# Token blocks of 480 columns that run across batch ends, in a kernel of polysketch attention followed by a SwiGLU block

## The chip, the cores and the metric

The kernel runs on one core of one Trainium2 chip. The metric is device time in microseconds (us), the median of several runs; lower is better. The profile is one execution of the same kernel, recorded by the hardware. Its engines are called PE (TensorE, matrix products), PEld (TensorE's weight loads), DVE (VectorE), ACT (ScalarE), POOL (GpSimd) and SP (SyncE, which here only issues DMAs).

## The reference

Attention with polynomial sketches, without a softmax, and then a gated feed-forward block over all tokens:

```python
batch, n_heads, seq, head_dim = (4, 4, 1088, 32)      # r = 8
def phi(x):
    a = np.einsum('rd,bhsd->bhsr', S1, x)
    b = np.einsum('rd,bhsd->bhsr', S2, x)
    return np.einsum('bhsi,bhsj->bhsij', a, b).reshape(*x.shape[:-1], r * r)
q_p, k_p = (phi(q), phi(k))
kv = np.einsum('bhsf,bhsd->bhfd', k_p, v)
z = np.sum(k_p, axis=2)
num = np.einsum('bhsf,bhfd->bhsd', q_p, kv)
den = np.einsum('bhsf,bhf->bhs', q_p, z)[..., None] + 1e-06
...
x = attn_out.transpose(0, 2, 1, 3).reshape(4352, 128)
g = x @ w_gate                        # 128 x 1536
silu = g * (1.0 / (1.0 + np.exp(-g)))
val = x @ w_val
out = (silu * val) @ w_out            # 1536 x 128
```

## The kernel before, in words

All tokens lie in `xT`, 128 model dimensions by 4352 token columns, 1088 for each of the four batches. Attention fills it batch by batch, and the feed-forward part reads it in blocks of columns. A *unit* is one block with one of the twelve chunks of 128 hidden features: gate product, value product, silu, product of the two (a tile of `hbuf`). The *down* product (`down`, L966, its matmul at L972) adds up the twelve hidden tiles of a block in one PSUM bank, `acc`, some five units later. `store` (L997) then transposes the sum on DVE (L1001) and issues one output DMA for each of the four groups of 32 features (L1007).

Each batch is cut into blocks of 384, 384 and 320 columns (`plan`, L65). Batch 0 goes through attention and the feed-forward part first, with plain FP32 products (`unit`, L933, matmuls at L941). The loop at L1240 runs the other three batches: nine blocks, 108 units, counted by `y`; `line` (L964) is the order of the blocks. The last of the line has 384 columns, of which the last 128 are multiplied the other way round at the very end (`straight`, L985, matmul at L987).

In that loop most products are *cut* (`cut_unit`, L889): tokens and weights are split into parts of fewer bits so that three faster F32R matmuls replace one FP32 matmul. One of them (L898) makes a small correction that ACT copies out of PSUM (L902); two more (L906, L907) accumulate the main part, which DVE adds to the correction (L908). Then ACT applies silu (L914) and POOL multiplies gate and value (L919). With `both=True` gate and value are cut. Otherwise only the value is, and the gate is one FP32 matmul (L900). The prediction calls the first kind *both* and the second *single*. Before, a unit is both from `y=26` (`GATES`) on and at y = 11, 14, 17, 20 and 23.

`cut_tokens` (L861) makes the parts of a block's tokens in three steps, x1 on ACT (L869), x0 on POOL or DVE (L870), and xd on DVE (L874); `cut_weights` (L828) does the same for weights, and its last gate part is the tile `gphq` (L859). In the loop `cut_tokens` is called in two halves, nine and four units before a block's first unit; the second half is xd.

PSUM has eight banks. `bank` and `pair` take the ones that were used longest ago and are not held; a both unit takes two pairs of the three that are left.

Attention of the later batches is written as a generator (`attentions`, L603) whose steps `parts_of` takes between units, by a rule on `y` (L1255). Its larger groups of matmuls wait at a `yield "pe"` until `group()` starts them, at the units listed in `GROUPS`. For batch 2: values and key sketches, then query sketches; for batch 3: numerators of batch 2 (L770) and values (L376), then query sketches (L330); last the numerators of batch 3. `numerators` copies its result into `xT` (L787). The steps between are DVE work above all: `query_step` (L732) makes the denominators (L737 to L743), multiplies query features (`phq`, L365) and transposes them (L752) into `phT`, which the numerators need.

Each engine works through its instructions in the order in which the code issues them.

Of the kernel before, what the change touches and what calls it, by code (L numbers as in the profile page):

```python
# [19 lines left out]
def kernel(  # L20
# [44 lines left out]
    plan = [(HX + 2 - s) // 3 for s in range(3)]  # L65
    XS = plan[0]
    steps = [(sum(plan[:s]), n) for s, n in enumerate(plan)]
    blocks = [(S * b + 64 * x0, 64 * n) for b in range(B) for x0, n in steps]
    BW = 64 * XS

    LAST = len(blocks) - 2
    SPLIT = BW - P

    thirds = [(c, c + 3) for c in range(0, NCH, 3)]
    pieces = dict.fromkeys(("wg", "wv"), [(0, 1), (1, 3)] + thirds[1:])
# [223 lines left out]

    NH = 27  # L300
    hbuf = const.tile([P, NH, BW], FP32, name="hbuf")
    slots = list(range(NH))
    slot_of = {}

    xT = const.tile([P, NT], FP32, name="xT")
# [297 lines left out]
    def attentions():  # L603

        yield from turn_keys(1)
        yield from turn_queries(1)
        hold("a")
        kp = wide("a")  # L610
        for i, c in enumerate(kpieces):
            key_products(kp[:, i, :], *c)
        ka = apool.tile([P, NC * H, R], FP32, tag="kas", name="kas")

        def sketch(ps, i):
            c0, c1 = kpieces[i]
            return ps[:, i, 0 : 64 * (c1 - c0)].rearrange("p (x t r) -> p x t r", t=2, r=R)

        for i, (c0, c1) in enumerate(kpieces):
            nc.scalar.copy(ka[:, H * c0 : H * c1, :], sketch(kp, i)[:, :, 0, :])  # L620
        phk = apool.tile([P, NC, H, R, R], FP32, tag="phk", name="phk")
        for n, (i, c0, c1) in enumerate(((0, 0, 3), (0, 3, 5), (1, 5, 7), (1, 7, 9))):
            first = H * (c0 - kpieces[i][0])
            kb = sketch(kp, i)[:, first : first + H * (c1 - c0), 1, :]
            key_features(phk, (ka[:, H * c0 : H * c1, :], kb), c0, c1)
            if n == 3:
                release("a")
            if n % 3 != 1:
                yield
        zs, sums = feature_sums(phk)  # L630
        for f in sums:
            f()
        yield from turn_keys(2)
        kvz = wide("a")
        values(kvz[:, 0, :], phk, zs)
        kab, kcopies = sketched(wide("b"), key_products, 2, "kab2")
        fold(kvz[:, 0, :])
        spread = spread_out(1, kvz[:, 0, :])
        hold("a", "b")
        yield  # L640
        qab, copies = sketched(wide("a"), query_sketches, 3, "qab")
        run_copies(copies, 2)
        yield
        run_copies(kcopies, 2)
        release("a", "b")
        for n, _ in enumerate(query_step(1, qab)):
            if n % 2 == 0:
                yield
        yield
        yield  # L650
        numerators(1, spread)
        yield "first"

        phk = apool.tile([P, NC, H, R, R], FP32, tag="phk", name="phk")
        yield from features(phk, kab)
        zs, sums = feature_sums(phk)
        for f in sums:
            f()
        yield from turn_keys(3)
        yield from turn_queries(2)  # L660
        for b in (2, 3):
            yield "pe"
            if b == 3:
                numerators(2, spread)
            hold("a")
            kv = bank()
            kv_bank = [max(used, key=used.get)]
            release("a")
            values(kv, phk, zs)
            if b == 2:  # L670
                kab, copies = sketched(wide("a"), key_products, 2, "kab2")
                run_copies(copies, 2)
            fold(kv)
            spread = spread_out(b, kv)
            touch(*kv_bank)
            yield
            yield "pe"
            qab, copies = sketched(wide("b"), query_sketches, 3, "qab")
            run_copies(copies, 2)
            yield  # L680
            if b == 2:
                yield from turn_queries(3)
                phk = hbuf[:, NH - 6 :, :].rearrange("p s (n h i j) -> p (s n) h i j", h=1, i=R, j=R)
                phk = phk.rearrange("p (c h) o i j -> p c (h o) i j", h=H)
                yield from features(phk, kab)
                zs, sums = feature_sums(phk)
            yield from beside(query_step(b, qab), sums)
        yield "pe"
        numerators(3, spread)
        yield  # L690
# [39 lines left out]
    turned = {}  # L730

    def query_step(b, qab):  # L732
        phq = apool.tile([P, NC, H, R, R], FP32, tag="phqs", name="phq")
        phT = turned[b] = apool.tile([P, H, 2, NC, 32], FP32, tag="phk", name="phT")
        dot = apool.tile([P, NC * H, R], FP32, tag="dot", name="dot")
        den = apool.tile([P, NC * H], FP32, tag="den", name="den")
        nc.vector.tensor_tensor(  # L737
            out=dot[:], in0=qab[:, 1, :, :], in1=qab[:, 2, :, :], op=ALU.mult
        )
        nc.vector.tensor_reduce(out=den[:], in_=dot[:], axis=AX.X, op=ALU.add)  # L740
        nc.vector.tensor_scalar_add(den[:], den[:], 1e-6)
        nc.vector.reciprocal(den[:], den[:])
        nc.vector.tensor_tensor(  # L743
            out=qab[:, 0, :, :], in0=qab[:, 0, :, :],
            in1=den[:].unsqueeze(2).to_broadcast([P, NC * H, R]), op=ALU.mult,
        )
        yield
        for c0, c1 in fpieces:
            x = slice(H * c0, H * c1)
            key_features(phq, (qab[:, 0, x, :], qab[:, 1, x, :]), c0, c1)  # L750
            yield
            nc.vector.transpose(  # L752
                out=phT[:, :, :, c0:c1, :].rearrange("p h g c t -> p c (h g) t"),
                in_=phq[:, c0:c1, :, :, :].rearrange(
                    "p c h (g i) j -> p c (h g) (i j)", g=2
                ),
            )
            yield
# [102 lines left out]
    def cut_tokens(i, engine=nc.gpsimd):  # L861
# [1 line left out]
        t0, n = blocks[i]  # L863
        x = xT[:, t0 : t0 + n]
        x1, x0, xd = x_parts[i] = [
            apool.tile([P, BW], F32R, tag=tag, name=name, bufs=2)
            for tag, name in (("qb", "x1"), ("dT", "x0"), ("rd", "xd"))
        ]
        nc.scalar.activation(x1[:, 0:n], x, AF.Copy, scale=CUT)  # L869
# [11 lines left out]
    def doubles(k):  # L881

        if room[1] + k > 2:
            room[:] = fpool.tile([P, 2, BW], FP32, tag="sgl", name="sum", bufs=4), 0
        at = room[1]
        room[1] += k
        return room[0][:, at : at + k, :]

    def cut_unit(i, j, both=False):  # L889
# [20 lines left out]
        )  # L910

        def last():
            sg = fpool.tile([P, BW], FP32, tag="sg", name="sg", bufs=5)[:, 0:n]
            nc.scalar.activation(sg, sums[:, 0] if both else g, AF.Silu)  # L914
            slot_of[i, j] = slots.pop(0)
            hj = hbuf[:, slot_of[i, j], :]
            hidden[i, j] = hj
            todo.append((i, j))
            nc.gpsimd.tensor_tensor(out=hj[:, 0:n], in0=sg, in1=sums[:, len(ws) - 1], op=ALU.mult)  # L919
# [13 lines left out]
    def unit(i, j, late=False, between=(None, None)):  # L933
# [4 lines left out]
        for o, w in ((g, wg), (u, wv)):  # L938
# [2 lines left out]
            nc.tensor.matmul(  # L941
                o[:, 0:n], w[:, j, :], xT[:, t0 : t0 + n], start=True, stop=True
            )
        sg = doubles(1)[:, 0, :] if late else fpool.tile([P, BW], FP32, tag="sg", name="sg", bufs=5)
        nc.scalar.activation(sg[:, 0:n], g[:, 0:n], AF.Silu)  # L945
        slot_of[i, j] = slots.pop(0)
        hj = hbuf[:, slot_of[i, j], :]
        hidden[i, j] = hj
        todo.append((i, j))
        if late:  # L950
# [10 lines left out]
        o, sg = lates.pop(0)  # L961
        nc.gpsimd.tensor_tensor(out=o, in0=o, in1=sg, op=ALU.mult)

    line = [3 * b + k for b in range(1, B) for k in ((0, 2, 1) if b == B - 1 else range(3))]  # L964

    def down():  # L966

# [17 lines left out]
    def straight(ps, j):  # L985

        nc.tensor.matmul(  # L987
            ps,
            hidden.pop((LAST, j))[:, SPLIT:BW],
            wo[:, j, :],  # L990
            start=(j == 0),
            stop=(j == NCH - 1),
        )
# [3 lines left out]
    def store(i, n):  # L997
        t0 = blocks[i][0]

        o = fpool.tile([P, BW // 32, 32], FP32, tag="o", name="o", bufs=2)  # L1000
        nc.vector.transpose(  # L1001
            out=o[:, 0 : n // 32, :], in_=acc.pop(i)[:, 0:n].rearrange("p (x t) -> p x t", t=32)
        )
        b, x0 = divmod(t0 // 32, NX)
        for a in range(4):
            queue = nc.scalar if i == LAST and a % 2 else nc.sync
            queue.dma_start(  # L1007
                out=rows[b, a, :, x0 : x0 + n // 32, :],
                in_=o[32 * a : 32 * a + 32, 0 : n // 32, :],
            )  # L1010

    keep_warm(98, 32)
    keep_warm(12, 64)
# [205 lines left out]
        parts_of(1)  # L1221
    run(x_steps or cut_tokens(HEAD, nc.vector))

    slots[:] = range(NH - 10)

    END = len(line) * NCH
    GROUPS, GATES = (5, 7, 26, 28, 52), 26

    token_steps = {}
    for m, i in enumerate(line[1:], 1):
        gen = cut_tokens(i)
        for at in (NCH * m - 9, NCH * m - 4):
            token_steps.setdefault(at, []).append(gen)
    oldest[0] = True
    hold("acc")
# [2 lines left out]
    for y in range(END):  # L1240
# [5 lines left out]
        if y == END - 1:  # L1246
            finish()
            unit(i, j)
        else:
            cut_unit(i, j, both=y >= GATES or (y > 10 and y % 3 == 2))  # L1250
        for _ in range(2):

            if len(todo) > min(5 + (todo[0] == (line[1], 0)), END - y + 1):
                down()
        parts_of(y < 8 or (y % 3 != 2 if y < GATES else y % 3 == 0))  # L1255
        if y == 0:
            gate_rows = cut_weights(wg, lows, nc.vector)
        for n, row in enumerate(gate_rows):
# [47 lines left out]
```

## Time and profile before

| what | value |
|---|---|
| median of 3 runs | 289.59 us (289.50 to 289.62) |
| span of the profiled execution | 287.6 us |
| granted TensorE clock | 1.000 |
| loop over later batches: first L898 to last L987 | 92.8 to 283.9 us |
| busy in it: DVE from 92.8 to 142.0 | 42.8 of 49.2 us |
| busy from 192.0 to 284.1 | DVE 55.9 of 92.1 us |
| HBM read, written | 11.41 MB, 2.23 MB |

The costliest groups of instructions of the loop, from the page's fifth part (columns: line, engine, operation, out<-in with partitions x elements, count, then busy us and mean ns, then the idle time of the engine before them and what ended it):

```profile
L919 POOL TENSOR_TENSOR hbuf<-sg,sum 128x384 f32<-128x384 f32 (+1 forms) x107 | 107.6, 1011 | 59.0 <-ACT sg L914 54.7
L908 DVE SCALAR_TENSOR_TENSOR sum<-PS,sum 128x768 f32<-128x768 f32 (+3 forms) x107 | 88.5, 830 | 46.7 <-ACT sum L902 41.0
L972 PE MATMUL PS<-hbuf,wo 128*128 128x384 f32 (+2 forms) x288 | 103.7, 459 | 0.0
L902 ACT ACTIVATE sum<-PS 128x768 f32<-128x768 f32 (+3 forms) x107 | 76.5, 714 | 43.7 <-PE PS L898 40.0
```

TensorE's matmuls overlap in the record (the next one starts before the one before has ended), so their durations are longer than their share of the time; the spacing of their starts is what they cost. An FP32 matmul shows as two halves.

### The profile page before, as it was taken

The numbers are of one execution on the slowest core, as the hardware profiler recorded it, in microseconds if no ns is written. First come the engines' busy times: TensorE is split into PE (matmuls) and PEld (weight loads), VectorE is DVE, ScalarE is ACT, GpSimd is POOL, SyncE is SP. The second block draws the span as 40 slices with busy tenths as digits, with TensorE's granted clock in tenths as the row PEclk, the third lists the DMA queues.
The fourth block names the chain that finished last, engine by engine and source line by source line (L and its number), as shares of the span: only waits on it lengthen the run. The fifth ranks groups of instructions, "written<-read, shape, count | busy, mean of one in ns | idle before, by whom it ended". The sixth has DMA issues, their size and how long they took to land.

```text
span 287.6 us, 6035 instructions
## 1 busy us (share of the span) xinstructions
PE 278.8 (97%) x2308; PEld 212.1 (74%) x2308; DVE 205.8 (72%) x337; ACT 173.3 (60%) x347; POOL 162.3 (56%) x183
## 2 busy tenths in 40 slices
PE   7899999999999999999998999999999999999995
PEld 7545566666666776777776888868888988889984
DVE  3997988884576979998548888746656567575651
ACT  3567565723402866665556787757777776777760
POOL 3315322279401894889924686555666676766660
PEclk9999999999999999999999999999999999999999
DMA  6574293212311213010001001001001010010101
GB/s 190 162 217 112 57 287 108 89 68 82 95 25 26 64 52 84 0 28 0 2 16 29 2 0 23 2 0 31 0 0 27 2 24 1 2 27 1 18 7 27
DMA packets 26141, 14.32 MB, mean 50 GB/s; under 512 B 19840, under 2 KB 24192, under 8 KB 26112
## 3 DMA queue, kind: packets, MB, share of 16 engines
q1 hardware_dynamic: 25456, 13.84, 18.7%
q8 instruction: 18, 0.29, 0.4%
q10 hardware_dynamic: 656, 0.10, 0.2%
q14 instruction: 11, 0.09, 0.1%
HBM read 11.41 MB, written 2.23 MB: 47 GB/s over the span
## 4 chain that ended last, share of the span: by engine, by line
PE 88%; DVE 6%; DMA 1%; ACT 1%; issue 1%; SPq 0%; DVEq 0%; ACTq 0%
PE PS L972 26%; PE PS L941 16%; PE PS L898 11%; PE PS L906 10%; PE PS L907 10%; PE PS L900 4%; PE PS L770 2%; PE PS L342 2%; PE PS L330 2%; PE PS L376 2%; DVE sum L908 1%; DMA kld<-in_k_dram 1%; PE PS L987 1%; DVE gphq L859 1%; PE PS L485 1%
## 5 line engine op out<-in xcount | busy, mean ns | idle before, releaser
L919 POOL TENSOR_TENSOR hbuf<-sg,sum 128x384 f32<-128x384 f32 (+1 forms) x107 | 107.6, 1011 | 59.0 <-ACT sg L914 54.7
L908 DVE SCALAR_TENSOR_TENSOR sum<-PS,sum 128x768 f32<-128x768 f32 (+3 forms) x107 | 88.5, 830 | 46.7 <-ACT sum L902 41.0
L972 PE MATMUL PS<-hbuf,wo 128*128 128x384 f32 (+2 forms) x288 | 103.7, 459 | 0.0
L902 ACT ACTIVATE sum<-PS 128x768 f32<-128x768 f32 (+3 forms) x107 | 76.5, 714 | 43.7 <-PE PS L898 40.0
L972 PEld LDWEIGHTS PS<-hbuf,wo 128*128 128x128 f32 x288 | 51.8, 189 | 9.8 <-issue 0.4
L898 PE MATMUL PS<-xd,gphq 128*128 128x384 f32 (+1 forms) x86 | 49.6, 576 | 1.7 <-DVE sum L908 1.3
L914 ACT ACTIVATE sg<-sum 128x384 f32<-128x384 f32 (+1 forms) x86 | 42.4, 493 | 5.5 <-DVE sum L908 5.3
L906 PE MATMUL PS<-x,w 128*128 128x384 f32 (+1 forms) x107 | 41.0, 384 | 0.0
L898 PE MATMUL PS<-xd,wd 128*128 128x384 f32 (+1 forms) x107 | 38.1, 356 | 0.2 <-DVE xd L874 0.2
L907 PE MATMUL PS<-x,wb 128*128 128x384 f32 (+1 forms) x107 | 35.1, 328 | 0.0
L941 PE MATMUL PS<-xT,wg 128*128 128x384 f32 (+1 forms) x74 | 29.5, 480 | 0.0
L941 PE MATMUL PS<-xT,wv 128*128 128x384 f32 (+1 forms) x74 | 28.8, 471 | 0.2 <-DVE wv L276 0.2
L906 PE MATMUL PS<-x,graw 128*128 128x384 f32 (+1 forms) x86 | 28.1, 326 | 0.2 <-ACT xT L787 0.2
L898 PEld LDWEIGHTS PS<-xd,wd 128*128 128x128 f32 x107 | 20.3, 190 | 10.5 <-issue 0.7
L907 PE MATMUL PS<-x,graw 128*128 128x384 f32 (+1 forms) x86 | 28.0, 326 | 0.0
L945 ACT ACTIVATE sg<-PS 128x384 f32<-128x384 f32 (+1 forms) x31 | 14.4, 467 | 21.3 <-PE PS L941 19.6
L898 PEld LDWEIGHTS PS<-xd,gphq 128*128 128x128 f32 x86 | 16.3, 189 | 12.3 <-DVE sum L908 2.3
L956 DVE TENSOR_TENSOR hbuf<-sg,PS 128x384 f32<-128x384 f32 (+1 forms) x31 | 16.2, 525 | 10.4 <-PE PS L941 10.1
L907 PEld LDWEIGHTS PS<-x,wb 128*128 128x128 f32 x107 | 20.1, 188 | 2.7
L906 PEld LDWEIGHTS PS<-x,w 128*128 128x128 f32 x107 | 20.1, 188 | 2.7
L941 PEld LDWEIGHTS PS<-xT,wv 128*128 128x128 f32 x74 | 13.8, 190 | 9.2 <-DVE hbuf L956 0.9
L941 PEld LDWEIGHTS PS<-xT,wg 128*128 128x128 f32 x74 | 13.3, 189 | 9.3 <-issue 1.2
(131 smaller groups left out, 351.6 us busy)
## 6 DMA issues: line engine op xcount, KB each, us to landing
kld<-in_k_dram SPq DMA_DIRECT2D x4, 544.0 KB, 4.1
vld<-in_v_dram SPq DMA_DIRECT2D x12, 144.0 KB, 4.7
qld<-in_q_dram SPq DMA_DIRECT2D x3, 544.0 KB, 3.3
raw<-in_moe_w_out_dram SPq DMA_DIRECT2D x4, 384.0 KB, 4.6
out_dram<-o SPq DMA_DIRECT2D x28, 48.0 KB, 1.9
raw<-in_moe_w_gate_dram SPq DMA_DIRECT2D x3, 384.0 KB, 3.2
raw<-in_moe_w_val_dram SPq DMA_DIRECT2D x3, 384.0 KB, 3.5
out_dram<-o SPq DMA_DIRECT2D x16, 40.0 KB, 1.7
```

The source lines that it names most:

```text
L898: nc.tensor.matmul(ds[:, k], wd, xd, start=True, stop=True)
L900: nc.tensor.matmul(g, wg[:, j, :], xT[:, t0 : t0 + n], start=True, stop=True)
L902: nc.scalar.activation(sums, ds, AF.Copy, scale=-1.0 / BETA)
L906: nc.tensor.matmul(ps[:, k], w1, x1, start=True, stop=False)
L907: nc.tensor.matmul(ps[:, k], wb, x0, start=False, stop=True)
L908: nc.vector.scalar_tensor_tensor(out=sums, in0=ps, scalar=1.0 + 1.0 / BETA, in1=sums, op0=ALU.mult, op1=ALU.add)
L914: nc.scalar.activation(sg, sums[:, 0] if both else g, AF.Silu)
L919: nc.gpsimd.tensor_tensor(out=hj[:, 0:n], in0=sg, in1=sums[:, len(ws) - 1], op=ALU.mult)
L941: nc.tensor.matmul(o[:, 0:n], w[:, j, :], xT[:, t0 : t0 + n], start=True, stop=True)
L945: nc.scalar.activation(sg[:, 0:n], g[:, 0:n], AF.Silu)
L956: nc.vector.tensor_tensor(out=hj[:, 0:n], in0=sg[:, 0:n], in1=u[:, 0:n], op=ALU.mult)
L972: nc.tensor.matmul(acc[i][:, 0:n], wo[:, j, :], hidden[i, j][:, 0:n], start=(j == 0), stop=(j == NCH - 1),)
```

## The change

The later batches' 3264 columns are cut into blocks of 480 from column 1088 on, across the ends of batches: six of 480 and one of 384. Tiles of the loop grow from 384 to 480 columns (`WB`); hidden tiles are slices of 480 columns of the same `hbuf`, 13 in place of 17. A store whose block runs across a batch's end issues its DMAs for each batch. Attention's groups move from units 5, 7, 26, 28, 52 to 4, 6, 20, 22, 40, and the first both unit to 20, with none before. Steps of attention are taken at every unit before 20 and at every second one after. The tokens of the third and the fifth block are cut later than the others, at 20 and 22, and at 40 and 44, since they hold columns of a batch whose numerators come at 20 or 40. `query_step` has one more `yield`, after the sum of the denominators, and a `phq` tile of a third of the size, which the three pieces share; for batch 1 the rule `n % 2` is turned over, so that its steps come where they came before.

```diff
-    blocks = [(S * b + 64 * x0, 64 * n) for b in range(B) for x0, n in steps]
+    blocks = [(64 * x0, 64 * n) for x0, n in steps]
     BW = 64 * XS
-    LAST = len(blocks) - 2
-    SPLIT = BW - P
+    WB = 480
+    blocks += [(t, min(WB, NT - t)) for t in range(S, NT, WB)]
+    LAST = len(blocks) - 1
+    SPLIT = blocks[LAST][1] - P
...
-            if n % 2 == 0:
+            if n % 2 == 1:
                 yield
...
     def query_step(b, qab):
-        phq = apool.tile([P, NC, H, R, R], FP32, tag="phqs", name="phq")
...
         nc.vector.tensor_reduce(out=den[:], in_=dot[:], axis=AX.X, op=ALU.add)
+        yield
         nc.vector.tensor_scalar_add(den[:], den[:], 1e-6)
...
-            x = slice(H * c0, H * c1)
-            key_features(phq, (qab[:, 0, x, :], qab[:, 1, x, :]), c0, c1)
+            x, n = slice(H * c0, H * c1), c1 - c0
+            phq = apool.tile([P, NC // 3, H, R, R], FP32, tag="phqs", name="phq")
+            key_features(phq, (qab[:, 0, x, :], qab[:, 1, x, :]), 0, n)
...
-            apool.tile([P, BW], F32R, tag=tag, name=name, bufs=2)
+            apool.tile([P, WB], F32R, tag=tag, name=name, bufs=2)
...
-    line = [3 * b + k for b in range(1, B) for k in ((0, 2, 1) if b == B - 1 else range(3))]
+    line = list(range(HEAD, len(blocks)))
...
-        b, x0 = divmod(t0 // 32, NX)
-        for a in range(4):
+        t1 = t0 + n
+        while t0 < t1:
+            b, x0 = divmod(t0 // 32, NX)
+            m = min(t1 - t0, S * (b + 1) - t0) // 32
+            k = (t0 - blocks[i][0]) // 32
+            for a in range(4):
...
-    slots[:] = range(NH - 10)
+    flat = hbuf[:].rearrange("p s w -> p (s w)")
+    slots[:] = [flat[:, WB * k : WB * k + WB] for k in range((NH - 10) * BW // WB)]
...
-    GROUPS, GATES = (5, 7, 26, 28, 52), 26
+    GROUPS, GATES = (4, 6, 20, 22, 40), 20
...
-        for at in (NCH * m - 9, NCH * m - 4):
+        for at in {2: (20, 22), 4: (40, 44)}.get(m, (NCH * m - 9, NCH * m - 4)):
             token_steps.setdefault(at, []).append(gen)
...
-            cut_unit(i, j, both=y >= GATES or (y > 10 and y % 3 == 2))
+            cut_unit(i, j, both=y >= GATES)
...
-        parts_of(y < 8 or (y % 3 != 2 if y < GATES else y % 3 == 0))
+        parts_of(y < GATES or y % 2 == 0)
```

More of the change, by code (lines that the diff above doesn't have):

```diff
@@ L301 @@
     hbuf = const.tile([P, NH, BW], FP32, name="hbuf")
-    slots = list(range(NH))
+    slots = [hbuf[:, k, :] for k in range(NH)]
     slot_of = {}
@@ L753, in query_step @@
                 out=phT[:, :, :, c0:c1, :].rearrange("p h g c t -> p c (h g) t"),
-                in_=phq[:, c0:c1, :, :, :].rearrange(
+                in_=phq[:, 0:n, :, :, :].rearrange(
                     "p c h (g i) j -> p c (h g) (i j)", g=2
@@ L883, in doubles @@
         if room[1] + k > 2:
-            room[:] = fpool.tile([P, 2, BW], FP32, tag="sgl", name="sum", bufs=4), 0
+            room[:] = fpool.tile([P, 2, WB], FP32, tag="sgl", name="sum", bufs=4), 0
         at = room[1]
@@ L912, in last @@
         def last():
-            sg = fpool.tile([P, BW], FP32, tag="sg", name="sg", bufs=5)[:, 0:n]
+            sg = fpool.tile([P, WB], FP32, tag="sg", name="sg", bufs=5)[:, 0:n]
             nc.scalar.activation(sg, sums[:, 0] if both else g, AF.Silu)
             slot_of[i, j] = slots.pop(0)
-            hj = hbuf[:, slot_of[i, j], :]
+            hj = slot_of[i, j]
             hidden[i, j] = hj
@@ L943, in unit @@
             )
-        sg = doubles(1)[:, 0, :] if late else fpool.tile([P, BW], FP32, tag="sg", name="sg", bufs=5)
+        sg = doubles(1)[:, 0, :] if late else fpool.tile([P, WB], FP32, tag="sg", name="sg", bufs=5)
         nc.scalar.activation(sg[:, 0:n], g[:, 0:n], AF.Silu)
         slot_of[i, j] = slots.pop(0)
-        hj = hbuf[:, slot_of[i, j], :]
+        hj = slot_of[i, j]
         hidden[i, j] = hj
@@ L988, in straight @@
             ps,
-            hidden.pop((LAST, j))[:, SPLIT:BW],
+            hidden.pop((LAST, j))[:, SPLIT : SPLIT + P],
             wo[:, j, :],
@@ L998, in store @@
         t0 = blocks[i][0]
-        o = fpool.tile([P, BW // 32, 32], FP32, tag="o", name="o", bufs=2)
+        o = fpool.tile([P, WB // 32, 32], FP32, tag="o", name="o", bufs=2)
         nc.vector.transpose(
@@ L1003, in store @@
         )
-        b, x0 = divmod(t0 // 32, NX)
-        for a in range(4):
[L1006 to L1010, printed above, removed]
+        t1 = t0 + n
[4 more added lines that the diff above has]
+            for a in range(4):
+                queue = nc.scalar if i == LAST and a % 2 else nc.sync
+                queue.dma_start(
+                    out=rows[b, a, :, x0 : x0 + m, :],
+                    in_=o[32 * a : 32 * a + 32, k : k + m, :],
+                )
+            t0 += 32 * m
     keep_warm(98, 32)
```

## The prediction

> **What bounds the kernel now.** I read the page first: the busy shares, the slices, the chain's totals.
>
> ```profile
> PE 278.8 (97%) x2308; PEld 212.1 (74%) x2308; DVE 205.8 (72%) x337; ACT 173.3 (60%) x347; POOL 162.3 (56%) x183
> PE   7899999999999999999998999999999999999995
> DVE  3997988884576979998548888746656567575651
> PE 88%; DVE 6%; DMA 1%; ACT 1%; issue 1%; SPq 0%; DVEq 0%; ACTq 0%
> ```
>
> TensorE carries the end. Only its own work, or a wait that stops it, moves the time. So I split the stretch in which the diff works: from unit y=0 (first matmul of L898, 92.75 us) to the last matmul of L987 (283.9). I add up each unit's matmuls from the spacing of their starts. The chain in order of time gives the spacing; two steady units of 384 columns and two of 320:
>
> ```profile
> 174.61 0.65 PE PS L972 x2
> 176.30 0.65 PE PS L972 x2
> ...
> 160.33 0.54 PE PS L972 x2
> 161.76 0.54 PE PS L972 x2
> ```
>
> A unit with both products cut ("both") takes 1.69 us at 384 columns, 1.42 at 320. It is six F32R matmuls (two each of L898, L906, L907) and one FP32 matmul of L972, which the trace shows as two halves of 0.32 us. In the timeline neighbouring F32R starts are 0.1745 us apart at 384 and 0.1465 at 320; 6 x 0.1745 + 0.645 = 1.692 and 6 x 0.1465 + 0.538 = 1.417, so the parts agree with the whole. A unit with the gate uncut ("single") has three F32R and one more FP32 matmul (L900): 1.168 + 0.645 = 1.81 at 384.
>
> Before there are 19 singles of 384, 2 of 320, 52 boths of 384, 34 of 320 and the last unit in FP32 (1.935): 34.5 + 3.0 + 88.0 + 48.2 + 1.9 = 175.6 us. (The last block's shorter downs and the extra matmuls of L987 cancel; both kernels have them.) The stretch is 191.1. Of the other 15.5, attention's matmuls take 10.2 (2.35 and 1.81 at the first two groups, 4.5 at the next two, 1.5 at the last). About 5 is waiting. The waits of TensorE from 92 to 285 us name the visible part:
>
> ```profile
> PE PS L898 <- DVE sum L908: 1.3, 1, 1.3
> PE PS L330 <- DVE sum L908: 0.5, 1, 0.5
> PE PS L898 <- DVE gphq L859: 0.4, 1, 0.4
> PE PS L906 <- ACT xT L787: 0.2, 1, 0.2
> PE PS L898 <- DVE xd L874: 0.2, 1, 0.2
> ```
>
> Counted by unit length against the sums above, the losses are larger than these rows: 0.7 at y=11 (gphq), 1.0 at y=25 to 28 (second row included), 1.6 at y=32 (first row), 1.3 around the last group at y=52. The biggest is a block of five instructions on VectorE; its timeline and TensorE's next start:
>
> ```profile
> 154.10 0.86 DVE L737 TENSOR_TENSOR dot<-qab 128x288 f32<-128x288 f32 x1
> 154.99 0.45 DVE L740 TENSOR_REDUCE den<-dot 128x36 f32<-128x288 f32 x1
> 155.47 0.61 DVE L741 TENSOR_SCALAR den<-den 128x36 f32<-128x36 f32 x1
> 156.12 0.38 DVE L742 RECIPROCAL den<-den 128x36 f32<-128x36 f32 x1
> 156.53 0.46 DVE L743 TENSOR_TENSOR qab<-qab,den 128x288 f32<-128x288 f32 x1
> 157.78 0.41 PE L898 MATMUL PS<-xd,gphq 128*128 128x320 f32 x1 [1.31 <-DVE sum L908]
> ```
>
> For 2.9 us L908 cannot empty PSUM, and the units behind it find no bank.
>
> **What the Trainium skill says.** "TensorE: Matmul & The Clock Gate", section "Wait — 56ns, not 53.3ns?": warm starts are N / 2.4 GHz plus about 2.5 ns apart. The FP32 halves agree (768 / 2.4 = 320, measured 322). The F32R ones do not: 160 + 14.5 and 133.3 + 13, so the trace's numbers are used. "Perfetto Trace Analysis", section "Matmuls", says larger matmuls are more efficient; 14 ns a matmul is all that can be won here. "SBUF — State Buffer", section "SBUF: two separate sides": a VectorE instruction with two SBUF inputs and a GpSimd one exclude each other. The trace agrees: xd (two SBUF inputs) takes from 476 to 1358 ns:
>
> ```profile
> L874 DVE SCALAR_TENSOR_TENSOR xd<-x,x x9: 476/953/1358, 92.1 to 256.4; 128x384 fp32r<-128x384 f32 x6, 128x320 fp32r<-128x320 f32 x3
> ```
>
> **The change, part by part.**
> 1. *Seven blocks for nine.* 108 units become 84: y=0 to 19 single at 480, 20 to 71 both at 480, then 11 boths and the last at 384. No row shows 480 columns. An F32R matmul is at least 200 + 13 = 213 ns and at most, on the straight line through 146.5 and 174.5, 216.5; I take 215 (the rest grew little over 64 columns). An FP32 one: 4 x 480 / 2.4 + 5 = 805. Single 3 x 0.215 + 2 x 0.805 = 2.255, both 6 x 0.215 + 0.805 = 2.095. Sum: 45.1 + 108.9 + 18.6 + 1.9 = 174.6, so **-1.0** (-1.7 at 213, -0.45 at 216.5). It is small because uncut gates cover 9600 columns instead of 7936, each one array pass more: 1664 / 2.4 = 0.7 of a gross 1.7.
> 2. *No both before y=20.* The first need of gphq moves from y=11 to y=20, 45 us after y=0 instead of 21; L859 issues at the same y (6 to 9). The wait goes: **-0.7** (0.4 to 0.7).
> 3. *Denominators in two parts.* For batch 3, dot and reduce (1.31) now fall at y=22 and the rest (1.45) at y=24, each before another L908. A 480 unit gives VectorE 2.1 us against about 1.17 of L908 (0.822 at 640 and 0.954 at 768 elements, so 1.03 ns an element, with 960), so 1.3 fits before a bank is missed. But the tokens of the block from y=24 on now get their xd at y=22, in VectorE's queue straight behind dot and reduce. Counted from the start of unit 22: the copies of qab (1.14) hold ACT, L902 ends at 1.6, L908 at 2.8, dot and reduce at 3.7 to 4.1, xd at 4.4 to 5.4. Unit 24's first matmul wants it at 4.2. Estimated new wait 0.2 to 1.2, taken 0.8; the queue behind it (L908 of y=23) is wanted only at 6.3. Net 0.8 - 1.6 = **-0.8** (-1.5 to +0.4).
> 4. *Start.* x1, x0 and xd of the first block grow by 96 columns each, in one chain (0.52, 0.56, 0.55 at 384): 3 x 0.09, and TensorE already waits 0.18 there: **+0.3** (0.2 to 0.5).
> 5. *Groups at 4, 6, 20, 22, 40.* Same attention work. In columns done they come at 0.97 to 1.07 of the old places; values at y=4 come 5.8 us after y=0, as before. The waits for banks at the second b=3 group and the last grow with L908: **+0.1** (-0.2 to 0.4).
> 6. *Costed at nothing:* fewer cut_tokens (six after the first, for eight) run beside TensorE. The smaller phq makes each feature wait for the transpose before it: some 0.1 twice at 80 us, hidden by the downs, which keep TensorE busy to 92.6. Block ends inside a batch add four store DMAs twice on SP, 0.5 us each at y=41 and 65: nothing that TensorE needs follows them closely (the ring copies of spread are issued at y=20). Thirteen slots for seventeen: six are in use at a time. The tail has the same 384 block. ACT at 480 needs about 0.97 + 0.59 of 2.095, GpSimd about 1.22: both fit.
>
> Sum: -1.0 - 0.7 - 0.8 + 0.3 + 0.1 = -2.1 on the span of 287.6, 285.5. The three runs (289.50 to 289.62) lie 2.0 above that span, so 289.6 - 2.1 = **287.5**.
>
> **Rivals.**
> *The wait only changes its name* (0.14): xd stops TensorE for as long as the denominators did and the matmul price is the upper one: -0.45 - 0.7 + 0.2 + 0.3 + 0.1 = -0.5, 289.0. For: xd has run up to 1.36 us beside GpSimd. Against: it needs both bad ends.
> *Everything hides* (0.12): xd comes in time, matmuls at 213: -1.7 - 0.7 - 1.5 + 0.3 = -3.6, 286.0. For: 0.2 is one end of my own count. Against: qab's copies lie in ACT's way.
> *VectorE is late to numerators(2)* (0.12), the slower side. Batch 2's tokens are wanted at y=20 with the last transpose at y=18. From y=6 to 18 VectorE has 13 L908 (0.62), four gphq (3.3), qT 1.5, features 4.1, denominators 2.45, phq and transposes 6.5, xd 1.6, store 0.7: 28.3 us, against 13 units and a sketch group of 31.1. It decides once these instructions stretch by more than 10%; each further 10% stops TensorE for 2.8. At 20% that gives 287.5 + 2.8 = 290.3. For: DVE shows 9 in these slices. Against: single units without the five boths leave it more room (42.8 busy of the 49.2 us from y=0 to 142 now).
>
> **How the numbers follow.** My case has 0.62, with 286.6 to 288.4 as its own range. 0.2% is 0.58 us, about what can be told from no change. Faster: 0.62, 0.12 and a third of the first rival, 0.78. Same 0.10, slower 0.12. The range, 286.2 to 289.2, leaves out the slower case and part of the best.
>
> **What would show it.** Right: boths 2.09 to 2.10 apart, no wait for gphq, no wait of L898 for L908 near y=24 to 26, but one for xd of 0.2 to 1.2 before y=24. Wrong: spacing above 2.11, any wait before numerators at y=20, or waits that return every second unit from 20 to 38, where queries' parts fall.

## The result, and the profile after

The changed kernel takes 288.29 us (median of 4 runs, 288.18 to 288.79) where the kernel before takes 289.61 beside it. The ratio is 0.9954, with a 95% interval from 0.9937 to 0.9971: 0.8 to 1.8 us faster, 1.3 in the middle. The forecast was faster by 2.1, 287.5 with a range of 286.2 to 289.2.

The page of the changed kernel, same lines as for before (line numbers after L65 move by 3 to 8; L898 is now L902, L908 is L912, L972 is L976):

```profile
PE 278.4 (97%) x2117; PEld 188.7 (66%) x2117; DVE 202.7 (71%) x309; ACT 165.7 (58%) x297; POOL 156.2 (55%) x157
PE   7899999999999999999999999999999999999994
DVE  3997988975595977999658889646656655675641
PE 89%; DVE 5%; ACT 2%; DMA 2%; issue 1%; SPq 0%; DVEq 0%; ACTq 0%
```

191 matmul records fewer, and TensorE is busy for 278.4 us instead of 278.8. That is the first sign that fewer, wider matmuls gave next to nothing. The slice in which PE stood at 8 before (the twenty-second of forty) stands at 9. The waits of TensorE from 92 to 285 us (us in total, how often, the longest):

```profile
PE PS L902 <- DVE xd L878: 1.0, 2, 0.5
PE PS L910 <- ACT xT L791: 0.2, 1, 0.2
```

The waits for the denominators' L908, for gphq and ahead of a sketch group are gone; two waits for xd of half a microsecond stand in their place, one before y=0 (it was 0.2) and one before y=24. At y=24 xd stands behind the first part of the denominators in VectorE's queue:

```profile
149.40 1.16 DVE L912 SCALAR_TENSOR_TENSOR sum<-PS,sum 128x960 f32<-128x960 f32 x1 [2.79 <-ACT sum L906]
150.48 1.01 DVE L739 TENSOR_TENSOR dot<-qab 128x288 f32<-128x288 f32 x1
...
151.52 0.45 DVE L742 TENSOR_REDUCE den<-dot 128x36 f32<-128x288 f32 x1
151.89 0.65 DVE L878 SCALAR_TENSOR_TENSOR xd<-x,x 128x480 fp32r<-128x480 f32 x1
...
152.59 0.48 PE L902 MATMUL PS<-xd,gphq 128*128 128x480 f32 x1 [0.51 <-DVE xd L878]
```

And the spacing of units, from the chain in order of time, in the third block and in the sixth:

```profile
164.80 0.81 PE PS L976 x2
166.93 0.81 PE PS L976 x2
169.06 0.81 PE PS L976 x2
```

```profile
239.57 0.81 PE PS L976 x2
241.68 0.81 PE PS L976 x2
243.78 0.81 PE PS L976 x2
```

A both unit of 480 columns takes 2.127 us in some blocks and 2.107 in others, never the 2.095 of the forecast.

To say where the time went I split the stretch from the first matmul of y=0 to the last of the loop's end in both traces. Every unit's matmuls count at the spacing measured for their size (F32R 146.5, 174.5 and, between the two kinds of block, 218 ns at 320, 384 and 480 columns; a half of an FP32 matmul 269, 322 and 402). What a unit takes beyond that is attention or waiting.

| us | before | after | difference |
|---|---|---|---|
| the units' matmuls | 175.6 | 175.7 | +0.1 |
| first two groups of attention (y=4 to 7, now 3 to 6) | 4.2 | 4.4 | +0.2 |
| gphq at y=11 | 0.7 | 0 | -0.7 |
| numerators and values of the second pair of groups | 3.3 | 3.4 | +0.1 |
| query sketches, and the wait ahead of them | 2.3 | 1.5 | -0.9 |
| y=30 to 36, now 23 and 24 (denominators, xd) | 1.7 | 0.8 | -0.9 |
| last group | 2.8 | 2.8 | -0.1 |
| whole stretch | 191.1 | 189.1 | -2.0 |
| from the first key product (L342) to y=0 | 86.8 | 87.1 | +0.3 |
| from the end of the last matmul to the end of the program | 3.5 | 3.8 | +0.3 |

Pieces below 0.1 are left out of the rows; they change the difference by 0.2. From the first key product on it is -1.7 to the last matmul and -1.4 to the end of the program, close to the 1.3 of the medians. The last row is not chance: the end takes 3.84 to 3.99 us in the recorded executions of all eight kernels with blocks of 480 and 3.54 to 3.57 in those of all five with the old ones. The spans (287.6 and 286.6) differ by only 1.0 because the first key product starts 0.33 us later in the recorded execution of the changed kernel. I take that for chance, since nothing in the change touches it, but it is not shown: it starts at 5.97 to 6.26 us in the recorded executions with the old blocks, at 6.10 to 6.61 in those with the new ones.

### The profile page after: what moved, and what is told of

Its sections match the earlier page's. It is cut to its first block, busy times and chain, and to the rows that moved or that the text cites. A ratio compares the mean times of both kernels' runs of the same rounds, so it can differ in the third digit from the quotient of the medians.

```text
span 286.6 us, 5490 instructions
## 1 busy us (share of the span) xinstructions
PE 278.4 (97%) x2117; PEld 188.7 (66%) x2117; DVE 202.7 (71%) x309; ACT 165.7 (58%) x297; POOL 156.2 (55%) x157
## 3 DMA queue, kind: packets, MB, share of 16 engines
HBM read 11.41 MB, written 2.23 MB: 48 GB/s over the span
## 4 chain that ended last, share of the span: by engine, by line
PE 89%; DVE 5%; ACT 2%; DMA 2%; issue 1%; SPq 0%; DVEq 0%; ACTq 0%
PE PS L976 28%; PE PS L945 16%; PE PS L902 11%; PE PS L910 10%; PE PS L911 10%; PE PS L904 5%; PE PS L774 2%; PE PS L333 2%; PE PS L345 2%; DMA kld<-in_k_dram 2%; PE PS L379 1%; DVE sum L912 1%; PE PS L991 1%; PE PS L488 1%; PE PS L436 1%
## 5 line engine op out<-in xcount | busy, mean ns | idle before, releaser
L923 POOL TENSOR_TENSOR hbuf<-sg,sum 128x480 f32<-128x480 f32 (+1 forms) x83 | 103.3, 1249 | 60.2 <-ACT sg L918 52.9
L912 DVE SCALAR_TENSOR_TENSOR sum<-PS,sum 128x960 f32<-128x960 f32 (+2 forms) x83 | 83.5, 1006 | 48.3 <-ACT sum L906 42.5
L906 ACT ACTIVATE sum<-PS 128x960 f32<-128x960 f32 (+2 forms) x83 | 70.9, 854 | 51.0 <-PE PS L902 50.9
L976 PE MATMUL PS<-hbuf,wo 128*128 128x480 f32 (+3 forms) x240 | 100.3, 517 | 0.0
L976 PEld LDWEIGHTS PS<-hbuf,wo 128*128 128x128 f32 x240 | 45.0, 189 | 13.1 <-issue 0.9
L902 PE MATMUL PS<-xd,gphq 128*128 128x480 f32 (+1 forms) x63 | 44.8, 711 | 0.5 <-DVE xd L878 0.5
L910 PE MATMUL PS<-x,w 128*128 128x480 f32 (+1 forms) x83 | 38.6, 465 | 0.0
L918 ACT ACTIVATE sg<-sum 128x480 f32<-128x480 f32 (+1 forms) x63 | 36.5, 580 | 0.6 <-DVE sum L912 0.6
L902 PE MATMUL PS<-xd,wd 128*128 128x480 f32 (+1 forms) x83 | 35.8, 431 | 0.5 <-DVE xd L878 0.5
L911 PE MATMUL PS<-x,wb 128*128 128x480 f32 (+1 forms) x83 | 31.3, 378 | 0.0
L902 PEld LDWEIGHTS PS<-xd,wd 128*128 128x128 f32 x83 | 15.7, 189 | 15.5 <-issue 14.6
L910 PE MATMUL PS<-x,graw 128*128 128x480 f32 (+1 forms) x63 | 23.6, 374 | 0.2 <-ACT xT L791 0.2
L911 PE MATMUL PS<-x,graw 128*128 128x480 f32 (+1 forms) x63 | 23.4, 371 | 0.0
L902 PEld LDWEIGHTS PS<-xd,gphq 128*128 128x128 f32 x63 | 11.8, 188 | 13.7 <-issue 11.1
```

The costliest lines, as they stand in the source:

```text
L902: nc.tensor.matmul(ds[:, k], wd, xd, start=True, stop=True)
L906: nc.scalar.activation(sums, ds, AF.Copy, scale=-1.0 / BETA)
L910: nc.tensor.matmul(ps[:, k], w1, x1, start=True, stop=False)
L911: nc.tensor.matmul(ps[:, k], wb, x0, start=False, stop=True)
L912: nc.vector.scalar_tensor_tensor(out=sums, in0=ps, scalar=1.0 + 1.0 / BETA, in1=sums, op0=ALU.mult, op1=ALU.add)
L976: nc.tensor.matmul(acc[i][:, 0:n], wo[:, j, :], hidden[i, j][:, 0:n], start=(j == 0), stop=(j == NCH - 1),)
```

## The experiments

Two theories first. A, the prediction's: each F32R matmul costs 14 ns beside its columns, so blocks of 480 save. B: its cost grows with the columns, the blocks save next to nothing, and all that was won is waits removed. The runs after the fourth take the waits one by one.

**The price of a matmul by its width.** The changed kernel with this ahead of the last multiplications (the output is the same):

```diff
+    for width in (480, 448, 384, 320, 256):
+        for k in range(16):
+            nc.tensor.matmul(mb[:, 0:width], w_all[k], xs[k % 2][:, 0:width], start=True, stop=True)
```

> The changed kernel with 80 extra F32R matmuls ahead of the last multiplications: 16 each at 480, 448, 384, 320 and 256 columns, each with weights of its own, into a free bank (the output is unchanged). Theory A (the prediction: about 14 ns of fixed cost in each F32R matmul): starts 214, 201, 174.5, 147 and 121 ns apart. Theory B (cost in proportion to columns, 0.4545 ns each, nothing fixed): 218, 204, 174.5, 145.5 and 116. Time: some 13 us above the changed kernel in both.

Measured in mean, without the first spacing at 480 (407 ns, behind an FP32 matmul): 220, 203.8, 175.7, 146.7 and 118.7 ns. Two pairs of neighbours in the timeline, at 480 and at 384:

```profile
280.24 0.38 PE L1277 MATMUL PS<-x,w 128*128 128x480 f32 x1
280.46 0.38 PE L1277 MATMUL PS<-x,wb 128*128 128x480 f32 x1
...
286.14 0.34 PE L1277 MATMUL PS<-x,wb 128*128 128x384 f32 x1
286.31 0.34 PE L1277 MATMUL PS<-x,w 128*128 128x384 f32 x1
```

From 256 to 480 columns that is 101.3 / 224 = 0.452 ns a column, which leaves 3 ns at width zero. The extra matmuls use parts of the value weights only. In the units of the same block the starts are 219 to 220 ns apart behind such parts and 215 to 218 behind the other weights, 217 in mean; with 217 at 480 it would be 0.44 ns a column and 6 at width zero. Theory A's fixed 14 is out either way. B is nearer, but not exact: 118.7 lies between the two theories, and 220 above both. VectorE, ScalarE and GpSimd did nothing from 278.7 to 292 us, so it is not the other engines that slow the wide ones. The run took 302.04 us, with the extra matmuls.

**Denominators in two parts on the old blocks.**

```diff
         nc.vector.tensor_reduce(out=den[:], in_=dot[:], axis=AX.X, op=ALU.add)
+        if b == 3:
+            yield
         nc.vector.tensor_scalar_add(den[:], den[:], 1e-6)
```

> The kernel before, with the denominators of batch 3 alone in two parts. Both theories: the 1.6 us lost at y=32 fall to 0.2 to 0.8, so 0.8 to 1.4 us faster. If less than 0.4 is won, the block of five instructions was not what held L908.

289.10 us against 289.56, ratio 0.9987 (0.9979 to 0.9996): 0.4 won, less than the 0.8 to 1.4 expected. The trace tells why. The loss from y=30 to 36 fell from 1.7 to 0.3, as both theories said, but a wait that the kernel before did not have stands ahead of the last group:

```profile
186.64 0.81 PE L974 MATMUL PS<-hbuf,wo 128*128 128x384 f32 x2
188.95 1.57 PE L772 MATMUL PS<-phT,spread 32*32 32x288 f32 x64 [1.50 <-DVE phT L754]
```

One more step in a row that gets one step every third unit puts the last transpose at y=51, right before the numerators of y=52. The gain of 1.4 was real, and 0.9 of it was given back at the last group (2.8 before, 3.8 now) by the step's own place.

**No both unit before y=26 on the old blocks.**

```diff
-            cut_unit(i, j, both=y >= GATES or (y > 10 and y % 3 == 2))
+            cut_unit(i, j, both=y >= GATES)
```

> The kernel before with no both unit ahead of y=26. Both theories: the 0.7 us lost at y=11 to gphq go, and five gates of 384 columns in one FP32 matmul instead of three F32R cost 5 x 0.12 = 0.6: within 0.3 us of before. If the matmuls of these gates did not matter, 0.7 faster.

289.36 against 289.56, ratio 0.9994 (0.9985 to 1.0004): no difference that can be told, as expected. In the trace the 0.7 at y=11 is gone and the units' sum is 0.6 higher.

**Both edits on the old blocks.**

> The kernel before with both edits, the old blocks of 384 and 320 and the old groups. Theory A: the seven blocks are worth 1.65 us of matmuls over this kernel, less 0.3 at the start, so this is 1.3 or more slower than the changed kernel: 289.6 or above. Theory B: the blocks are worth at most 0.4 in matmuls, less 0.3 at the start, and the sketch group's wait (0.7) is left: 288.4 to 289.0.

288.88 us, ratio 0.9977 (0.9968 to 0.9986): inside B's window, 0.7 below A's bound. But the wait for phT is in here too, so the comparison of A and B is made again below without it.

**The changed kernel with the denominators in one piece.**

```diff
-            if n % 2 == 1:
+            if n % 2 == 0:
                 yield
...
         nc.vector.tensor_reduce(out=den[:], in_=dot[:], axis=AX.X, op=ALU.add)
-        yield
```

> The changed kernel with the denominators in one piece again. They now stand ahead of xd in VectorE's queue at y=22, so if the split is what keeps xd's wait at 0.5, the wait before y=24 grows by the 1.45 us of the second part: 1.2 to 1.5 slower than the changed kernel, 289.5 to 289.8. If 480-column units give VectorE room enough by themselves (the rival: the blocks, not the split, removed the wait at y=32), less than 0.4 slower.

289.99 us, ratio to the kernel before 1.0021 (1.0008 to 1.0035), so slower than the changed kernel by more than the change had won; by the stretch of the trace, 1.6 (190.7 against 189.1). VectorE's timeline, and TensorE's waits:

```profile
150.32 1.01 DVE L739 TENSOR_TENSOR dot<-qab 128x288 f32<-128x288 f32 x1
151.36 0.45 DVE L742 TENSOR_REDUCE den<-dot 128x36 f32<-128x288 f32 x1
151.85 0.18 DVE L743 TENSOR_SCALAR den<-den 128x36 f32<-128x36 f32 x1
152.07 0.38 DVE L744 RECIPROCAL den<-den 128x36 f32<-128x36 f32 x1
152.48 0.92 DVE L745 TENSOR_TENSOR qab<-qab,den 128x288 f32<-128x288 f32 x1
153.32 0.65 DVE L877 SCALAR_TENSOR_TENSOR xd<-x,x 128x480 fp32r<-128x480 f32 x1
```

```profile
PE PS L901 <- DVE xd L877: 2.6, 2, 2.1
PE PS L909 <- ACT xT L790: 0.2, 1, 0.2
```

xd stands behind all five and TensorE waits for it for 2.1 us instead of 0.5. As long as xd is issued at y=22, the new blocks need the split: the rival, that wider units make room enough by themselves, is ruled out there. Whether they need it with xd issued earlier was not tried.

**xd of the third block one unit earlier.**

```diff
-        for at in {2: (20, 22), 4: (40, 44)}.get(m, (NCH * m - 9, NCH * m - 4)):
+        for at in {2: (20, 21), 4: (40, 44)}.get(m, (NCH * m - 9, NCH * m - 4)):
```

> The changed kernel with the third block's xd one unit earlier, at y=21, ahead of the sketch group, where VectorE stands idle for 2.8 us. If xd behind dot and reduce is the wait before y=24: the 0.5 goes and with it the 0.8 of that unit, 0.5 to 0.8 faster than the changed kernel. If L908's bank is what counts there: no change.

287.45 us, ratio to before 0.9918 (0.9904 to 0.9933): 0.8 faster than the changed kernel. VectorE had an idle stretch there, which xd now fills:

```profile
145.35 1.16 DVE L912 SCALAR_TENSOR_TENSOR sum<-PS,sum 128x960 f32<-128x960 f32 x1 [0.16 <-ACT sum L906]
146.42 1.22 DVE L878 SCALAR_TENSOR_TENSOR xd<-x,x 128x480 fp32r<-128x480 f32 x1
149.30 1.16 DVE L912 SCALAR_TENSOR_TENSOR sum<-PS,sum 128x960 f32<-128x960 f32 x1 [1.66 <-ACT sum L906]
```

No loss is left at y=23 and 24. The order of VectorE's queue was all of it.

**Both units at 11, 14 and 17 in the changed kernel**, the line of the kernel before put back.

> The changed kernel with units 11, 14 and 17 both, as the kernel before had them. Three gates of 480 columns in three F32R matmuls (3 x 218) instead of one FP32 (804): 0.45 faster if gphq (issued at y=6 to 9) and VectorE keep up. By the prediction's rival, VectorE late to numerators: each adds 0.5 to a queue that was 39.5 of 43.6 us busy, and a wait before y=20 eats it: no change or slower.

Slower: ratio to before 1.0071 (1.0046 to 1.0097). Its times spread from 290.4 to 293.7, so I go by its trace: the stretch is 191.4 us, 2.3 more than the changed kernel's.

```profile
PE PS L902 <- DVE gphq L863: 1.8, 1, 1.8
PE PS L902 <- DVE xd L878: 1.0, 2, 0.5
PE PS L333 <- DVE sum L912: 0.6, 1, 0.6
PE PS L910 <- ACT xT L791: 0.2, 1, 0.2
```

The units' sum falls by the expected 0.45, but gphq comes 1.8 us late at y=11. It was not VectorE's load up to y=20 that decided, as the expectation had it: no wait ahead of the numerators appeared. The fourth gphq stands behind two key features of 2.3 us together in VectorE's queue:

```profile
118.28 2.28 DVE L368 TENSOR_TENSOR hbuf<-kab 128x512 f32<-128x512 f32 x2
...
120.48 0.54 DVE L863 SCALAR_TENSOR_TENSOR gphq<-hbuf,graw 128x384 fp32r<-128x384 f32 x1
...
121.08 0.48 PE L902 MATMUL PS<-xd,gphq 128*128 128x480 f32 x1 [1.84 <-DVE gphq L863]
```

A second wait came with it, ahead of the sketch group, which the changed kernel does not have (third row of the waits).

**The first block's xd ahead of the key features, too.** In the loop that ends batch 0 `next(x_steps, None)` is called twice in a row, so that xd follows x0 directly; with xd at y=21.

> As the run with xd at y=21, and the first block's xd ahead of the key features, right behind x0. If both waits of L902 for xd are the order of VectorE's queue: 0.5 more than that run alone, 1.0 to 1.3 faster than the changed kernel. If the first one only passes on to the values group at y=4, whose features come 0.65 later: as that run, or slower.

286.54 us, ratio 0.9896 (0.9876 to 0.9915): 1.75 faster than the changed kernel, 0.9 more than the run with xd at y=21 alone. More than the 0.5 expected: from the last down of batch 0 to y=0 TensorE's starts lie 0.03 us apart, where the changed kernel has 0.89 and the kernel before 0.61; 0.15 of it comes back in y=0's own matmuls. The changed kernel first, then this one:

```profile
92.20 0.70 PE L976 MATMUL PS<-hbuf,wo 128*128 128x320 f32 x2
93.36 0.46 PE L902 MATMUL PS<-xd,wd 128*128 128x480 f32 x1 [0.46 <-DVE xd L878]
```

```profile
92.25 2.05 PE L976 MATMUL PS<-hbuf,wo 128*128 128x320 f32 x7
93.89 0.63 PE L902 MATMUL PS<-xd,wd 128*128 128x480 f32 x1
```

The recorded execution of this run took 288.08 us; it lost 1.1 us ahead of the first gate product of batch 0, so its y=0 doesn't come earlier on the clock. In the last run below, which has the same edit, y=0 comes 0.85 us sooner after the first key product than in the changed kernel. So the kernel before lost about 0.4 there, not the 0.18 that its wait's row shows. The values group at y=4 did not get later.

**The kernel before without its waits for gphq and the denominators, on the old blocks.**

```diff
+        if b == 3:
+            yield
...
-            cut_unit(i, j, both=y >= GATES or (y > 10 and y % 3 == 2))
+            cut_unit(i, j, both=y >= GATES)
...
-        parts_of(y < 8 or (y % 3 != 2 if y < GATES else y % 3 == 0))
+        parts_of(y < 8 or (y % 3 != 2 if y < GATES else y % 3 == 0 or y == 31))
```

> The kernel before with its old blocks of 384 and 320 and old groups, no both ahead of y=26, the denominators of batch 3 in two parts, and the second part at y=31, so that no later step moves: the waits of y=11 and y=32 should go and no new one come. Set against the changed kernel with xd at y=21, which has neither. Theory A (each F32R matmul has 14 ns fixed): the blocks are worth 1.65, the sketch group's wait 0.6, less 0.5 at the start and the early groups: 1.7 slower than that one, 289.1. Theory B (cost in proportion to columns): 0.5 for columns of uncut gates as counted with measured spacings, 0.6 for the group, less 0.5: 0.6 slower, 288.0.

288.46 us, ratio 0.9955 (0.9941 to 0.9970): the gain of the whole change, without the blocks. Its waits:

```profile
PE PS L330 <- DVE sum L910: 0.5, 1, 0.5
PE PS L908 <- ACT xT L789: 0.2, 1, 0.2
PE PS L900 <- DVE xd L876: 0.2, 1, 0.2
```

Against the run with xd at y=21 it is 1.0 slower, between B's 0.6 and A's 1.7; the two intervals leave 0.5 to 1.7, so the times alone can't decide. The traces part them. The stretch is 1.5 us longer: its units' matmuls come to 176.2 us against 175.7, so the blocks are worth the 0.5 of B; the sketch group with its wait (first row) takes 0.9 more, and some 0.4 are small losses from y=32 to 36 that no theory had; the first groups take 0.2 less. At the start and at the end of the program the old blocks save 0.3 each.

**The two buffers of x1, x0 and xd changed over.** One unused tile of each kind is taken ahead of the first block.

> The changed kernel with one extra, unused turn of the two buffers of x1, x0 and xd, so that odd and even blocks change places in memory. If the place makes units of the third and fifth block take 2.127 and those of the second, fourth and sixth 2.107, the two change over. If something else does (the accumulator's bank, the weights), nothing changes.

288.24 us in one execution, as the changed kernel. But the blocks did change places:

| both unit of 480, median us | third block | fourth | fifth | sixth |
|---|---|---|---|---|
| changed kernel | 2.127 | 2.107 | 2.127 | 2.107 |
| buffers changed over | 2.107 | 2.127 | 2.107 | 2.127 |

The place of the token tiles in SBUF costs 20 ns a both unit. All three tiles changed places together, so which of them counts is open, and why one place is slower was not tried. It isn't the place alone: in single units the changed kernel takes 2.260 us in the first block and 2.273 in the second, and with the buffers changed over 2.260 in both.

**The last group one unit later.** The kernel with both xd early, with this on top:

```diff
-    GROUPS, GATES = (4, 6, 20, 22, 40), 20
+    GROUPS, GATES = (4, 6, 20, 22, 41), 20
...
-        for at in {2: (20, 21), 4: (40, 44)}.get(m, (NCH * m - 9, NCH * m - 4)):
+        for at in {2: (20, 21), 4: (41, 45)}.get(m, (NCH * m - 9, NCH * m - 4)):
```

> The kernel with both xd early and the last group at y=41 in place of 40 (the fifth block's tokens at 41 and 45). By the code's rotation of three bank pairs, the main pair of y=39 is the one that numerators need second, that of y=40 is not. If the 0.7 lost ahead of the last group is this pair waiting for L908's successor: 0.5 to 0.7 faster than with the group at 40. If it is the wait for xT's copies behind it: no change.

286.01 us (285.89 to 286.19), ratio to before 0.9867 (0.9846 to 0.9888): 0.5 faster than with the group at 40, and the fastest kernel here, 3.7 below the one before. The numerators now run through in 1.57 us; with the group at 40 they took 2.23, stopped in the middle until L912 had read the second bank pair. The group at 40, then at 41:

```profile
186.50 2.23 PE L774 MATMUL PS<-phT,spread 32*32 32x288 f32 x64
...
187.20 1.01 PEld L774 LDWEIGHTS PS<-phT,spread 32*32 32x32 f32 x60 [0.57 <-DVE sum L912]
```

```profile
187.20 1.57 PE L774 MATMUL PS<-phT,spread 32*32 32x288 f32 x64
```

From 92 to 285 us one wait of TensorE is left:

```profile
PE PS L910 <- ACT xT L791: 0.2, 1, 0.2
```

## Why the prediction was right, and where it was not

The sign and the range held, the range by luck in part: two errors of 1.1 and 0.7 us with opposite signs met, and a third term, the program's end, was not in the sum. Part by part:

*Part 1, seven blocks for nine: wrong.* Forecast -1.0, measured +0.1. The step that failed is the price of an F32R matmul at 480 columns: 215 ns taken, at most 216.5 allowed, 217 and 220 measured in the units (2.107 and 2.127 less 0.8045 for the down, over six). The 215 took what is left over the prediction's N / 2.4 GHz as nearly fixed, 13 ns at 320 columns and 14.5 at 384. It isn't: it grows from 12 ns at 256 columns to 17 in the one kind of block and 20 in the other at 480. The straight line through the two widths was nearly right for the first kind; that the place of the operands adds 3 ns in the second, no line through widths could show. Some 3 ns more on 372 matmuls, the six of 52 boths and the three of 20 singles, is the missing 1.1 us. 24 of the 52 boths lay above 2.11, which the prediction had named as a sign of being wrong. The other half of that step, uncut gates on 1664 more columns, was counted rightly as a loss, 0.5 by the measured spacings where it said 0.7.

*Part 2, gphq: right.* Forecast -0.7, measured -0.7. The early boths put back in the changed kernel show the wait return, larger (1.8). In the kernel before, the run without early boths gained nothing that can be told, because FP32 gates cost as much as the wait; the forecast had that cost in part 1.

*Part 3, denominators: right.* Forecast -0.8 with a new wait for xd of 0.8, measured -0.9 with 0.8 by the unit's length, 0.5 in the wait's row. xd finished 4.9 us after unit 22 began, in the middle of the forecast's 4.4 to 5.4. Putting the denominators back into one piece and moving xd both moved exactly this wait.

*Part 4, start: right,* +0.3. That TensorE lost only 0.18 there before was not: the runs with the early xd show about 0.4.

*Part 5, groups: the mechanism was named, its direction was not seen.* Forecast +0.1 with a range to -0.2, measured -0.6 for the groups together. The sketch group's wait for a bank did not grow with L908; it vanished, since after y=21 the pair that L912 reads last is not the one that the sketches write. This is a matter of counting the turns of the pairs, which the code alone allows, and the forecast did not count. Worked through with the code's rule (the bank used longest ago), it hangs on one bank: in the changed kernel the values at y=20 get a bank outside the three pairs that the boths use. In the kernel before (at y=26), and in the changed kernel with early boths, they get a bank of a pair; the turn of the pairs shifts by one, and the sketches find theirs still being read. The traces agree: 0.5 and 0.6 us of wait in these two, none in the changed kernel. So this gain was luck, not aim. The last group moved to 41 shows the same rule on another group.

*Part 6, costed at nothing: held in the loop.* No wait for slots, stores or phq appeared. The tail was costed wrongly: its block has the same 384 columns, yet the program's end takes 0.3 us more. The last output lands 2.6 us after the last matmul in both kernels; GpSimd's closing instructions behind it come later. Why is open.

*The rivals.* The wait changed its name in part (0.8 of 1.7 by the units' length). Not everything hid: xd came late, and in no kind of block did the matmuls of 480 columns take as little as 213. VectorE late to the numerators did not happen, nor with early boths: there the queue's order stopped TensorE at y=11 first.

## What to carry to other kernels

Before you count on fewer and wider instructions, measure one at the width that you will use: two narrower ones left 213 to 216.5 ns open where 217 to 220 was true, and here that was the difference between 1 us and none. Where the bound engine is full, look for the few places where it stops, and read in the queue of the engine that it waits for what stands ahead: moving one xd by a unit won 0.8 us, two such moves and a group's turn won more than the whole change. A long piece that is split needs its last part in time as well: the same split won 1.4 us and gave 0.9 back where its row of steps ended one slot later.

## What the runs showed of the hardware that was not expected

F32R matmuls 128 x 128 by N, one behind the other, start 118.7, 146.7, 175.7, 203.8 and 220 ns apart at 256, 320, 384, 448 and 480 columns, at a granted clock of 0.999: 12, 13, 16, 17 and 20 ns over N / 2.4 GHz. FP32 matmuls keep to N x 4 / 2.4 GHz plus 5 (645 and 804 ns at 384 and 480). "TensorE: Matmul & The Clock Gate", section "Wait — 56ns, not 53.3ns?", gives N / 2.4 GHz plus 2.5 for a warm array; for F32R the runs here differ, by 15 to 18 ns at 480, and the measurement decides. And the same both unit takes 20 ns longer or shorter with its token tiles in one buffer or in the other.
